# Normalized rows turned by VectorE's 32x32 blocks and a DRAM scratch instead of TensorE's transposes

## The chip, the cores and the metric

The kernel runs on one core of a Trainium2 chip. That core has five engines with instruction queues of their own: TensorE (PE, with its weight loads PEld), VectorE (DVE), ScalarE (ACT), GpSimd (POOL) and SyncE (SP), which here only issues transfers. The transfers run on 16 DMA engines. SBUF is the on-chip memory of 128 partitions, PSUM the accumulator memory of 8 banks into which TensorE writes. The metric is the time of one execution on the device, in microseconds (us).

## What is computed

The reference is one block of a network on x with 2048 rows of 512 values, in f32: softmax attention with 32 heads of 16 values, then a gated MLP that mixes rows.

```python
def _A_ref(x, wqkv, wo):                       # attention, H = 32, Dh = 16
    qkv = (x @ wqkv).reshape(B, S, 3, H, Dh).transpose(2, 0, 3, 1, 4)
    p = softmax(einsum("bhqd,bhkd->bhqk", q, k) * Dh ** -0.5)
    o = einsum("bhqk,bhkd->bhqd", p, v)
    return o.transpose(0, 2, 1, 3).reshape(B, S, D) @ wo

def _B_ref(x, w_in, w_sp, b_sp, w_out):        # F = 1376, Fh = 688
    z = gelu(einsum("bsd,df->bsf", x, w_in))
    z1, z2 = z[..., :Fh], layernorm(z[..., Fh:])
    g = einsum("ts,bsf->btf", w_sp, z2) + b_sp[None, :, None]
    return einsum("bsf,fd->bsd", z1 * g, w_out)

h = x + _A_ref(layernorm(x), wqkv, wo)
out = h + _B_ref(layernorm(h), w_in, w_sp, b_sp, w_out)
```

Each f32 product is made of three products of rounded halves (hi and lo): hi x hi, hi x lo and lo x hi. To *split* a tile below is to make these two halves.

## The kernel before, in words

The 2048 rows are cut into 16 blocks of 128. The kernel has four stages: the projections to q, k and v; the attention; a middle stage, which makes h and z of every block; and the last stage, which mixes the blocks with w_sp and writes the output. The change lies in the end of the attention stage and in the middle stage.

The path of one block (`sb`) through the middle stage is this.

- `load_o` (line 619) asks, on SyncE's queue, for the attention output o of the block, already turned (from the scratch `o_scr`, 256 KB), for the reciprocals of the softmax sums `rc` (four transfers from `r_scr` that repeat each row 16 times), and for the rows of x (`xr`). GpSimd then multiplies o by rc (line 630). The buffers are o and rc two each, xr three.
- `split_o` (line 633) makes the halves of o, one on ScalarE and one on VectorE.
- `make_h` (line 645) is 12 products on TensorE (line 643); `add_h` (line 651) adds x on VectorE, stores h to `h_scr`, and takes statistics; `scale_h` (line 659) makes mean and scale from them.
- `hn`, the normalized row block, is made by ScalarE (line 1097), or by VectorE for the first three blocks (line 883).
- `turn` (line 1010) turns it: four transposes of 128x128 on TensorE (line 1015) into a PSUM tile `tp`, and a split of that tile to `hT`, first half on ScalarE (line 100), second on VectorE (line 105).
- `make_z` (line 1024), three times: 12 products each (lines 108 to 110) into a PSUM tile, and the gelu on ScalarE (line 1034).
- `gate_z` (line 1037) stores both halves of z by ScalarE's queue, normalizes the second (line 1046), calls what it is given as `meanwhile`, and, for blocks 8 to 15, lets GpSimd combine two blocks (lines 1058 to 1066) to the operands of the last stage. The second half of z has five buffers (line 1021).

The blocks are taken in the order 0, 1, 2, 8, 9, 10, 3, 11, 4, 12, 5, 13, 6, 14, 7, 15 (`h_rows`). Below, "row k" is the k-th in this order. Step k of the middle stage makes h of row k + 3, turns row k + 1, makes z of row k, splits o of row k + 4 and asks for o of row k + 5. h and hn of rows 0, 1 and 2 are made earlier, in the last part of the attention stage (`play_final` and `more_h`), where o of rows 3 and 4 is asked for too.

The order is written out by hand: in the last part of the attention stage the queues of TensorE, ScalarE, VectorE and SyncE, and from the middle stage on GpSimd's too, execute in the order of the program text. An instruction that waits holds up all that stands behind it on its engine. In the last part of the attention the order of pieces is the string `FINAL`: G is a score with its exponential, V a product with v, H one of the 12 products of h, T the transfers of the row maxima.

## Time and profile before

| | us |
|---|---|
| median of 3 runs | 1803.15 |
| lowest and highest | 1802.88, 1803.16 |
| the profiled execution | 1802.38 |
| its span | 1800.6 |

| engine | busy us | share of the span | instructions |
|---|---|---|---|
| TensorE (PE) | 1793.1 | 100% | 13371 |
| TensorE weight loads (PEld) | 1050.6 | 58% | 13371 |
| VectorE (DVE) | 1500.0 | 83% | 3034 |
| ScalarE (ACT) | 1378.4 | 77% | 2674 |
| GpSimd (POOL) | 218.4 | 12% | 299 |

The last part of the attention runs from about 1307 to 1351 us of the span, the middle stage from 1351 to 1514 us. The granted clock of TensorE is full throughout.

How to read the rows that follow. A row of the groups names line, engine and operation, then output and inputs with their shapes, the number of instructions, and after the bar the busy us, the mean ns of one, and the idle time of the engine before them with what ended it. A row of the timeline begins with the start and the duration in us; in brackets stands the idle time before it and its releaser. SPq and ACTq rows are transfers being issued on the queues of SyncE and ScalarE; how long the data then takes is not in them. A row of the windows gives for a stretch of time the busy us of PE, PEld, DVE, ACT and POOL with their instructions, the clock, the busy share of the DMA engines and GB/s.

### The profile page before, as it was taken

What the parts mean: (1) busy time and instruction counts of PE and PEld (TensorE: products, weight loads), DVE (VectorE), ACT (ScalarE), POOL (GpSimd) and SP (SyncE); (2) the same over time, 40 slices, a digit from 0 to 9 for tenths busy, and PEclk for the clock granted to TensorE, in tenths of its full rate; (3) what the DMA queues carried; (4) which work ended last, traced back from release to release, by engine and by line L of the source; (5) the groups of instructions that cost most, each with busy time, mean ns of one, the idle gap of its engine ahead of it and who ended that gap; (6) DMA issues with size and microseconds to landing.
All of it is one profiled execution on the core that took longest, in us unless ns stands there. A gap on an engine that the chain in (4) does not pass through costs nothing.

```text
span 1800.6 us, 36057 instructions
## 1 busy us (share of the span) xinstructions
PE 1793.1 (100%) x13371; PEld 1050.6 (58%) x13371; DVE 1500.0 (83%) x3034; ACT 1378.4 (77%) x2674; POOL 218.4 (12%) x299
## 2 busy tenths in 40 slices
PE   9999999999999999999999999999999999999999
PEld 6876444444444444444444444444448889999998
DVE  6487999999999999999999999999936676778664
ACT  3224999999999999999999999999994445334231
POOL 2241000011010100000000000000110754001111
PEclk9999999999999999999999999999999999999999
DMA  6677111221120111021012011100134554668562
GB/s 199 192 194 182 43 26 27 49 56 30 36 59 19 51 39 26 20 50 35 14 36 44 24 30 38 26 15 15 40 74 143 168 176 151 216 208 278 184 197 91
DMA packets 148184, 157.54 MB, mean 87 GB/s; under 512 B 63032, under 2 KB 93256, under 8 KB 146664
## 3 DMA queue, kind: packets, MB, share of 16 engines
q1 hardware_dynamic: 143224, 143.82, 29.6%
q10 hardware_dynamic: 4752, 11.41, 1.6%
q8 instruction: 105, 1.72, 0.4%
q14 instruction: 71, 0.58, 0.1%
q0 software_dynamic: 32, 0.01, 0.0%
HBM read 99.69 MB, written 54.56 MB: 86 GB/s over the span
## 4 chain that ended last, share of the span: by engine, by line
PE 99%; DVE 1%; DMA 0%; issue 0%; ACT 0%; DVEq 0%
PE pv L726 30%; PE s L700 10%; PE s L237 9%; PE m L700 9%; PE m L237 7%; PE acc L108 6%; PE acc L110 6%; PE acc L109 6%; PE g L110 4%; PE g L109 4%; PE g L108 4%; PE acc L643 2%; PE tp L1319 1%; PE h L643 1%; PE acc L1340 0%; PE tp L1015 0%
## 5 line engine op out<-in xcount | busy, mean ns | idle before, releaser
L704 ACT ACTIVATE pt<-s 128x512 f32<-128x512 f32 (+1 forms) x1149 | 668.5, 632 | 3.4 <-PE s L700 3.0
L726 PE MATMUL pv<-pt,vst 128*32 128x256 f32 (+1 forms) x6048 | 595.2, 467 | 0.0
L242 DVE TENSOR_REDUCE mx<-s 128x1 f32<-128x512 f32 x826 | 539.6, 682 | 42.3 <-PE s L237 34.4
L704 ACT ACTIVATE pt<-m 128x512 f32<-128x512 f32 x855 | 500.3, 616 | 0.2 <-PE m L700 0.2
L242 DVE TENSOR_REDUCE mx<-m 128x1 f32<-128x512 f32 x682 | 452.3, 682 | 28.3 <-PE m L237 21.2
L700 PE MATMUL s<-qst,kst 50*128 50x512 f32 x1193 | 418.5, 437 | 0.0
L237 PE MATMUL s<-kst,qst 48*128 48x512 f32 x963 | 343.7, 421 | 0.0
L700 PE MATMUL m<-qst,kst 50*128 50x512 f32 x855 | 340.1, 440 | 0.0
L237 PE MATMUL m<-kst,qst 48*128 48x512 f32 x794 | 290.8, 423 | 0.0
L700 PEld LDWEIGHTS s<-qst,kst 50*128 50x128 f32 x1193 | 187.4, 184 | 145.0 <-DVE mx L242 91.0
L726 PEld LDWEIGHTS pv<-pt,vst 128*32 128x32 f32 x6048 | 120.4, 108 | 217.6 <-issue 208.5
L700 PEld LDWEIGHTS m<-qst,kst 50*128 50x128 f32 x855 | 146.2, 184 | 129.4 <-DVE mx L242 88.9
L237 PEld LDWEIGHTS s<-kst,qst 48*128 48x128 f32 x963 | 166.8, 184 | 40.4 <-issue 12.8
L237 PEld LDWEIGHTS m<-kst,qst 48*128 48x128 f32 x794 | 137.1, 184 | 41.7 <-issue 15.2
L247 ACT ACTIVATE ab<-s 128x512 f32<-128x512 f32 x167 | 100.4, 601 | 14.2
L102 POOL CAST mparts<-nm 128x16 fp32r<-128x16 f32 x32 | 6.3, 196 | 861.3 <-DVE nm L255 861.3
L251 DVE CUSTOM_DVE_ANT_0 ab<-s,ab 128x512 f32<-128x512 f32 x137 | 93.2, 680 | 5.1 <-PE s L237 5.1
L955 ACT ACTIVATE ws<-a 128x512 fp32r<-128x512 f32 x80 | 45.7, 621 | 48.7 <-PE g L110 23.8
L251 DVE CUSTOM_DVE_ANT_0 ab<-m,ab 128x512 f32<-128x512 f32 x112 | 76.2, 680 | 4.9 <-PE m L237 4.9
L237 PE MATMUL s<-dst,qst 48*128 48x512 f32 x167 | 79.6, 477 | 0.0
L1034 ACT ACTIVATE z<-acc 128x464 f32<-128x464 f32 (+2 forms) x64 | 27.5, 456 | 63.5 <-PE acc L110 63.5
L108 PE MATMUL acc<-wi,hT 128*128 128x464 f32 (+2 forms) x196 | 72.8, 371 | 0.0
(219 smaller groups left out, 2586.9 us busy)
## 6 DMA issues: line engine op xcount, KB each, us to landing
a<-in_w_sp SPq DMA_DIRECT2D x80, 256.0 KB
qst<-q_scr SPq DMA_DIRECT2D x192, 64.0 KB
z_scr<-z ACTq DMA_DIRECT2D x32, 344.0 KB
kst<-k_scr SPq DMA_DIRECT2D x42, 256.0 KB
k_scr<-part SPq DMA_DIRECT2D x16, 512.0 KB
q_scr<-part SPq DMA_DIRECT2D x16, 512.0 KB
z<-z_scr SPq DMA_DIRECT2D x14, 344.0 KB
b<-z_scr SPq DMA_DIRECT2D x24, 172.0 KB
```

Source lines behind the costliest of these rows:

```text
L108: nc.tensor.matmul(ps, lh, rh, start=first, stop=False)
L109: nc.tensor.matmul(ps, lh, rl, start=False, stop=False)
L110: nc.tensor.matmul(ps, ll, rh, start=False, stop=last)
L237: nc.tensor.matmul(acc, q[r, p, c], keys[r, p], start=True, stop=True)
L242: nc.vector.reduce_max(at(t, e if t else e - 1), acc, axis=AX.X)
L247: nc.scalar.activation(ab[0], acc, AF.Relu)
L251: nc.vector.tensor_tensor_reduce(ab[0], acc, ab[0], 1.0, LOW, ALU.add, ALU.max, at(0, 0))
L643: yield nc.tensor.matmul(acc, o2[b][:, d, :], wo2[a][:, d, :], start=i == 0, stop=i == 3 * DB - 1)
L700: nc.tensor.matmul(out, kst[hg % 2][r, p, kb * P:(kb + 1) * P], qst[hg * NQ + qb][r, p, :], start=True, stop=True)
L704: nc.scalar.activation(out, scores, AF.Exp, scale=DH ** -0.5)
L726: nc.tensor.matmul(pv[0][32 * j:32 * j + 32, cols], vst[hg % 2][:, c:c + 32], pt[:, places[t, p], cols], start=kb == 0, stop=kb == NB - 1 ...
L955: nc.scalar.activation(hi, src, AF.Copy)
```

## The change

The rows of hn are no longer turned by TensorE. VectorE transposes each 32x32 block of the 128x512 tile in its place (`flip`); four transfers of SyncE write the result to a new DRAM scratch `ht_scr` in pieces of 32 values, so that the blocks come to stand in their turned places; one more transfer reads the turned block back (`fetch_turned`), and it is split from SBUF (`split_turned`).

In step k of the middle stage VectorE transposes row k + 3 behind the statistics of z, `meanwhile` issues the fetch of row k + 2, then the load of o, and last the four writes of row k + 3; row k + 1 is split behind the split of o. o is asked for six rows ahead, row k + 6 instead of k + 5, and o of row 5 at the start of the stage. Rows 0, 1 and 2 are transposed and written in the attention stage, rows 0 and 1 are fetched and row 0 is split there. The two PSUM buffers of `tp` go to the accumulators of `make_z`, which get seven instead of five.

```diff
@@ -90,6 +90,7 @@
     o_scr = dram.tile([D, S], F32, name="o_scr")
     r_scr = dram.tile([H, S], F32, name="r_scr")
     h_scr = dram.tile([S, D], F32, name="h_scr")
+    ht_scr = dram.tile([D, S], F32, name="ht_scr")
     z_scr = [dram.tile([S, FH], F32, name=f"z{i}_scr") for i in range(2)]
     s_scr = dram.tile([HB, P, HB, P], F32, name="s_scr")
     g_scr = [dram.tile([3, P, FC], F32, name=f"g{p}_scr") for p in range(HB)]
@@ -614,7 +615,7 @@
     wi4 = w_in.rearrange("(a p) c -> p a c", p=P)
 
     h_rows = [0, 1, 2, HB, HB + 1, HB + 2] + [sb + HB * i for sb in range(3, HB) for i in range(2)]
-    os_, o2s, xrs, hns, hTs = {}, {}, {}, {}, {}
+    os_, o2s, xrs, hTs = {}, {}, {}, {}
 
     def load_o(sb):
 
@@ -655,6 +656,33 @@
         nc.sync.dma_start(h_scr[sb * P:(sb + 1) * P, :], h)
         hst[sb] = e2.tile([P, 6], F32, name="st")
         nc.vector.bn_stats(hst[sb], h)
+
+    def flip(sb, hn):
+
+        z = e2.tile([P, D], F32, name="hz", tag="hn", bufs=3)
+        nc.vector.transpose(z, hn)
+        q = 32
+
+        def write():
+            for i in range(P // q):
+                c = sb * P + q * i
+                nc.sync.dma_start(ht_scr[:, c:c + q].rearrange("(j r) c -> r j c", r=q),
+                                  z[q * i:q * i + q, :].rearrange("r (j c) -> r j c", c=q))
+
+        return write
+
+    def fetch_turned(sb, pool, **slot):
+
+        raws[sb] = pool.tile([P, DB, P], F32, name="ht", **slot)
+        nc.sync.dma_start(raws[sb], ht_scr[:, sb * P:(sb + 1) * P].rearrange("(a p) s -> p a s", p=P))
+
+    def split_turned(sb, eh=None):
+
+        hTs[sb] = [hT[0][:, i, turns[0] % 2] for i in range(2)]
+        turns[0] += 1
+        split(hTs[sb][0], hTs[sb][1], raws.pop(sb), eh)
+
+    raws, turns, hT = {}, [0], []
 
     def scale_h(sb):
         mv = e2.tile([P, 2], F32, name="mv")
@@ -820,6 +848,8 @@
                             invert()
                         if len(units) in (7, 5):
                             load_o(h_rows[(7, 5).index(len(units)) + 3])
+                        if len(units) in (13, 3):
+                            fetch_turned(h_rows[(13, 3).index(len(units))], e2, tag="rc")
                     unit, pt, p = half
                     for step in score(unit, p, pt):
                         step()
@@ -864,7 +894,7 @@
 
             for _ in range(k):
                 if not pieces:
-                    sb = h_rows[len(hns)]
+                    sb = h_rows[made[0] // (3 * DB)]
                     acc = later[0].tile([P, 512], F32, name="h")
                     pieces.extend([sb, acc, h_products(sb, acc)])
                 sb, acc, products = pieces
@@ -873,15 +903,18 @@
                 if made[0] % (3 * DB):
                     continue
                 pieces.clear()
-                after = h_rows[len(hns) + 1]
+                if made[0] == 6 * DB:
+                    split_turned(h_rows[0])
+                after = h_rows[made[0] // (3 * DB)]
                 o = os_.pop(after)
                 hi, lo = o2s[after] = [e2.tile([P, DB, P], F32R, name=f"o2{i}", bufs=1) for i in range(2)]
                 nc.vector.tensor_copy(hi, o)
                 add_h(sb, acc, lambda: nc.vector.tensor_sub(lo, o, hi.bitcast(F32)))
                 mv, rs = scale_h(sb)
-                hns[sb] = e2.tile([P, D], F32, name="hn", bufs=3)
-                nc.vector.tensor_scalar(hns[sb], xrs.pop(sb), mv[:, 0:1], rs,
+                hn = e2.tile([P, D], F32, name="hn", bufs=3)
+                nc.vector.tensor_scalar(hn, xrs.pop(sb), mv[:, 0:1], rs,
                                         op0=ALU.subtract, op1=ALU.mult)
+                flip(sb, hn)()
 
         made = [0]
         units = [(hg, qb, kb) for hg in range(HG) for qb in range(NQ) for kb in range(NB)]
@@ -919,6 +952,7 @@
                 if n == 482:
                     split_o(h_rows[0], "pool", "pool")
             load_o(h_rows[2])
+            hT.append(wc.tile([P, 2, 2, DB, P], F32R, name="hT", tag="w2"))
             maxima.close()
             for stack in reversed(singles):
                 stack.close()
@@ -1000,22 +1034,8 @@
     with ExitStack() as mid:
         m2 = mid.enter_context(tc.tile_pool(name="mid_2", bufs=2))
         zs, zst = {}, {}
-        hT = wc.tile([P, 2, 2, DB, P], F32R, name="hT", tag="w2")
         ph = mid.enter_context(tc.tile_pool(name="mid_ph", bufs=1, space=PSUM))
-        pt = mid.enter_context(tc.tile_pool(name="mid_pt", bufs=2, space=PSUM))
-        ps = mid.enter_context(tc.tile_pool(name="mid_ps", bufs=5, space=PSUM))
-
-        turned = [0]
-
-        def turn(sb):
-
-            hn = hns.pop(sb)
-            tp = pt.tile([P, DB, P], F32, name="tp")
-            for d in range(DB):
-                nc.tensor.transpose(tp[:, d, :], hn[:, d * P:(d + 1) * P], ident)
-            hTs[sb] = [hT[:, i, turned[0] % 2] for i in range(2)]
-            turned[0] += 1
-            split(hTs[sb][0], hTs[sb][1], tp, "act")
+        ps = mid.enter_context(tc.tile_pool(name="mid_ps", bufs=7, space=PSUM))
 
         def new_z(sb):
             zs[sb] = [m2.tile([P, FH], F32, name=f"z{i}", bufs=1 + 4 * i) for i in range(2)]
@@ -1067,13 +1087,11 @@
 
         w = [Slot(wc, f"w{i}") for i in range(3)]
         row = dict(enumerate(h_rows))
-        turn(row[0])
+        load_o(row[5])
         for k in range(NB):
             sb, new = row[k], row.get(k + 3)
             if new is not None:
                 make_h(new, (ph if k else ps).tile([P, 512], F32, name="acc"))
-            if k + 1 < NB:
-                turn(row[k + 1])
             if new is not None:
                 mv, rs = scale_h(new)
                 nb = minus_mean(e2, mv, rs)
@@ -1089,16 +1107,28 @@
             make_z(sb, *chunks[0])
             if k + 4 < NB:
                 split_o(row[k + 4])
+            if k + 1 < NB:
+                split_turned(row[k + 1], "act")
             make_z(sb, *chunks[1])
             for c in range(2):
                 nc.vector.bn_stats(zst[sb][:, c, :], zs[sb][1][:, c * FC:(c + 1) * FC])
             if new is not None:
-                hns[new] = e2.tile([P, D], F32, name="hn", bufs=3)
-                nc.scalar.activation(hns[new], xrs.pop(new), AF.Identity, bias=nb, scale=rs)
+                hn = e2.tile([P, D], F32, name="hn", bufs=3)
+                nc.scalar.activation(hn, xrs.pop(new), AF.Identity, bias=nb, scale=rs)
+                write = flip(new, hn)
             for c in chunks[2:]:
                 make_z(sb, *c)
             hTs.pop(sb)
-            gate_z(sb, lambda: k + 5 < NB and load_o(row[k + 5]))
+
+            def meanwhile():
+                if k + 2 < NB:
+                    fetch_turned(row[k + 2], m2)
+                if k + 6 < NB:
+                    load_o(row[k + 6])
+                if new is not None:
+                    write()
+
+            gate_z(sb, meanwhile)
             if not k:
                 invert()
             if k == NB - 5:
```

## The prediction

> **What bounds the kernel now.** I read the page first: the busy shares and the chain that ended last.
>
> ```profile
> span 1800.6 us, 36057 instructions
> ...
> PE 1793.1 (100%) x13371; PEld 1050.6 (58%) x13371; DVE 1500.0 (83%) x3034; ACT 1378.4 (77%) x2674; POOL 218.4 (12%) x299
> ...
> PE 99%; DVE 1%; DMA 0%; issue 0%; ACT 0%; DVEq 0%
> ```
>
> TensorE is the chain for 99% of the span. So work taken from TensorE is worth its whole time, as long as everything that feeds TensorE keeps up with the shorter beat. Next the chain in order of time over the stage with the transposes. Its columns are start, us, what.
>
> ```profile
> 1351.36 0.59 PE tp L1015 x4
> ...
> 1383.99 2.76 PE acc L643 x12
> ...
> 1394.66 2.77 PE acc L643 x12
> ...
> 1498.67 0.44 PE tp L1015 x4
> ```
>
> A step with an output-projection row (12 products of L643, four transposes of L1015, 36 products of the gMLP input) lasts 1394.66 - 1383.99 = 10.67 us, with no gap. There are 16 groups of four transposes, the first costing 0.59 us and each later one 0.44 us of the chain. The busy time by step and the groups by line show what the other engines have to spare:
>
> ```profile
> 1383.99:1394.66 10.67, 10.67 (x54) 9.40 (x53) 7.30 (x25) 4.50 (x8) 1.28 (x1) 1.00 0.52 162
> ...
> L1015 PE MATMUL tp<-ident,hn 128*128 128x128 f32 x64 | 9.6, 273 | 0.0
> L135 DVE TENSOR_SCALAR rs_r<-rs_t 128x1 f32<-128x1 f32 x34 | 7.3, 214 | 1.2
> L281 DVE STREAM_TRANSPOSE mturned<-mparts 128x32 f32<-128x32 f32 x32 | 6.5, 204 | 0.6 <-DMA o<-o_scr 0.6
> L105 DVE TENSOR_TENSOR hT<-tp,hT 128x512 fp32r<-128x512 f32 x16 | 10.8, 678 | 5.8 <-ACT hT L100 5.8
> ```
>
> In that step (PE, PEld, DVE, ACT, POOL, clock, DMA share, GB/s) VectorE works 7.30 us, ScalarE 4.50, the DMA engines are 0.52 busy, and the clock is full.
>
> **What the change takes away.** All 64 transposes leave TensorE: 0.59 + 15 x 0.44 = **7.2 us** of the chain. The group's 9.6 us of busy time is an upper bound, because those matmuls overlap their neighbours. The full step becomes 10.67 - 0.44 = 10.23 us. Write S for the start of a step: step 0 still starts at 1351.36, and step k at 1351.36 + 10.23 k while nothing stalls. The splits of hT go on in the same number, and only move behind the split of o. PSUM goes from five and two buffers to seven for the gMLP accumulators, at no price.
>
> **What it adds on VectorE.** One 128x512 block transpose per row, which the trace does not show. It is new work, so no gain is in it: at least the 0.20 us of the 128x32 one, at most 16 times that, 3.26 us. A pass over one element costs 0.214 us (L135), so the 0.204 is nearly all a start that is paid once; I take 0.68 us, the pass over 512 elements. VectorE then has 8.0 of 10.23 us, and at 3.26 it has 10.6, hardly over a step. The place matters more: the transpose stands before the statistics of z, and there VectorE idles before the next add.
>
> ```profile
> 1390.86 0.69 DVE L105 TENSOR_TENSOR o<-o,o 128x512 fp32r<-128x512 f32 x1
> ...
> 1397.47 0.69 DVE L653 TENSOR_TENSOR xr<-acc,xr 128x512 f32<-128x512 f32 x1 [1.72 <-PE acc L643]
> ...
> 1334.27 0.43 DVE L879 CAST o<-o 128x512 fp32r<-128x512 f32 x1 [6.31 <-PE h L643]
> ...
> 1338.49 0.55 DVE L883 TENSOR_SCALAR hn<-xr,mv,rs_r 128x512 f32<-128x512 f32 x1
> ```
>
> The 1.72 us gap covers 0.68; without the cover the add is late by the excess, 1.5 us at 3.26, and what waits for the add is only the next row's statistics. The three transposes and the one split moved into the last attention stage lie in gaps like the 6.31 us before L879; without them ScalarE's exponentials would still not wait, as they read only scores.
>
> **What it adds on the queue of SyncE.** Per step four stores of 64 KB and one fetch of 256 KB. Order in a step: store of h, fetch of a turned row, o, four rc, x, and last the four stores, which wait for the transpose. The rows of before for step 3 on SyncE, and of the slow broadcast reads rc:
>
> ```profile
> 1387.51 0.33 SPq L655 DMA_DIRECT2D h_scr<-xr  x1
> 1387.93 0.39 SPq L623 DMA_DIRECT2D o<-o_scr  x1
> 1388.37 2.47 SPq L626 DMA_DIRECT2D rc<-r_scr  x4
> ...
> 1130.24 1.71 SPq L195 DMA_DIRECT2D raw<-v_scr  x2
> ...
> 1135.64 1.04 POOL L197 COPY vst<-raw 128x1024 f32<-128x1024 f32 x1 [12.22 <-DMA raw<-v_scr]
> ```
>
> At 2.47 / 4 = 0.62 us an issue, five more are 3.1 us beside the present 0.33 + 0.39 + 2.47 and 0.4 for x (as for o), 3.6: 6.7 of 10.23 us, so the queue fits. The stores of 2048 pieces of 128 bytes have no row. The nearest is raw: two loads, 4096 pieces of 128 bytes, and the reader starts 5.4 us after the first issue. I take that as the stores' landing too: issued from about S+9.9 (transpose done), landed by S+15.3, which is 5 us into the next step. The fetch behind them is read a step later, so it has some 8 us to spare.
>
> **Where the moved load bites.** The o of row k+6 goes into the buffer of row k+4, which comes free only when VectorE has made o's low half: 1390.86 + 0.69 is S+7.56, in the new beat S+7.1. Before, the row k+5 was asked for at S+3.9. GpSimd multiplies o by rc, and in its order that stands ahead of the gate work of the same step. So the gate work waits too. These are its rows, with the rows of ScalarE that need the buffers it frees:
>
> ```profile
> 1396.52 1.28 POOL L630 TENSOR_TENSOR o<-o,rc 128x512 f32<-128x512 f32 x1 [9.46 <-DMA rc<-r_scr]
> ...
> 1407.83 1.29 POOL L630 TENSOR_TENSOR o<-o,rc 128x512 f32<-128x512 f32 x1
> ...
> 1430.47 1.30 POOL L630 TENSOR_TENSOR o<-o,rc 128x512 f32<-128x512 f32 x1
> ...
> 1389.75 0.56 ACT L1034 ACTIVATE z<-acc 128x464 f32<-128x464 f32 x1 [1.93 <-PE acc L110]
> ...
> 1432.46 0.56 ACT L1034 ACTIVATE z<-acc 128x464 f32<-128x464 f32 x1 [1.92 <-PE acc L110]
> ...
> 1369.03 2.46 SPq L626 DMA_DIRECT2D rc<-r_scr  x4
> ...
> 1377.81 1.29 POOL L630 TENSOR_TENSOR o<-o,rc 128x512 f32<-128x512 f32 x1 [8.69 <-DMA rc<-r_scr]
> ```
>
> Call L the time from the last rc issue to the multiply: 1396.52 - 1390.84 = 5.7 us in step 3, 1377.81 - 1371.49 = 6.3 in step 1. Three gates in a row (steps 3, 4, 5) keep GpSimd busy from 1396.52 to 1430.47, 33.95 us. The z of step 7 takes the buffer that the third gate frees (five buffers, line 1021), and before it had 1432.46 - 1430.47 = 2.0 us to spare. New: the multiply of step 3 can start at S+7.1 + 2.9 (o and rc issues) + L; the third gate ends at S+43.95 + L; ScalarE wants the buffer at 4 x 10.23 + 5.32 (1389.75 is S+5.76, less 0.44) = S+46.24. So ScalarE waits w = L - 2.3: 3.4 us at L = 5.7. From that activation to o's low half is 1391.55 - 1389.75 = 1.8 us, and the next step's L643 needs it: it tolerates w = 10.23 - 5.32 - 1.8 = 3.1 us. The stall of TensorE is **L - 5.4**, once. Beyond about L = 6.6 the wait in step 5 also delays the o of row 11, and each further microsecond of L counts twice. For L the low end is 5.7 (stall 0.3; none if the reads come faster). The high end: the reads now share the DMA engines with two stores of z, x and the new stores. I take L = 6.5, near the rows, **1.1 us** of stall.
>
> ```profile
> z_scr<-z ACTq DMA_DIRECT2D x32, 344.0 KB
> ```
>
> With x and a turned row, 128x512 f32 each, that is 2 x 344 + 256 + 256 KB = 1.2 MB; at 162 GB/s per 0.52 share, 312 GB/s, all of it ahead of the reads is 4 us: L = 10.3, stall (10.3 - 5.4) + (10.3 - 6.6) = 8.6 us.
>
> **The start of the stage.** Row 5 is now asked for behind the stores of row 2 and the last attention output:
>
> ```profile
> 1350.99 0.55 DVE L883 TENSOR_SCALAR hn<-xr,mv,rs_r 128x512 f32<-128x512 f32 x1
> ...
> 1352.96 0.32 SPq L747 DMA_DIRECT2D o_scr<-o  x1
> ...
> 1357.94 0.51 SPq L748 DMA_DIRECT2D sums<-o  x1
> ...
> 1359.17 0.38 SPq L623 DMA_DIRECT2D o<-o_scr  x1
> ...
> 1370.26 0.68 DVE L105 TENSOR_TENSOR o<-o,o 128x512 fp32r<-128x512 f32 x1
> ```
>
> 1351.54 + 0.7 transpose + 4 x 0.62 issues = 1354.8, the eight transfers 5.5 us, so o at 1360.3, 1.1 us later than 1359.17; o's low half at 1370.94 + 1.1 = 1372.0 at worst, against S of step 2 at 1351.36 + 20.46 = 1371.8. I take **0.4 us**; with a 3.26 us transpose it is up to 2.8, and nothing if VectorE was not waiting for the load there.
>
> **Other loads behind the stores.** Row 4, in the attention stage, now waits for the stores of row 1: 1338.49 + 0.55 + 0.7 + 2.5 = 1342.2, then 2.9 + L + 1.3, ready at 1352.9; its split comes at 1351.36 + 5.9 = 1357.3. Four microseconds cover it. At the end of the stage the third block of spatial weights is issued behind the last stores:
>
> ```profile
> 1483.97 0.93 SPq L961 DMA_DIRECT2D a<-in_w_sp  x2
> ...
> 1490.91 2.54 POOL L975 TENSOR_TENSOR s<-a,a 128x512 f32<-128x512 f32 x2
> ...
> 1509.41 0.93 POOL L956 TENSOR_TENSOR n<-z,n 128x344 fp32r<-128x344 f32 x1
> ...
> 1513.97 0.32 PE L108 MATMUL g<-t,ws 128*128 128x344 f32 x1
> ```
>
> New issue: step 12 at 1474.1 + 12.4 + 1.5 of stalls = 1488, four microseconds later, so GpSimd's differences start about when they did, and its last gate ends near 1510.3 as now. The last stage then begins at 1513.97 - 5.7 = 1508.3, but with the first of that gate's four products; the one that ends at 1510.3 is the last. I put nothing; if TensorE waited for all of it, it is 2 us.
>
> **The sum**: -7.2 + 1.1 + 0.4 = **-5.7 us**. Against the profiled execution, 1802.38 us (1.8 beside its span), that is 1796.7; the median of the runs is 0.8 higher, 1803.15, so 1797.4 us.
>
> **Rival 1: the late multiply eats the gain.** Same mechanism, L of 7.7 to 9.5: stall 3.4 to 7.0 us, gain between 3.4 and -0.2. For it: the reads now run while z is stored. Against it: L was 6.3 at most where stores of z overlapped. Time at L = 8.5: stall 5.0, 1803.15 - 7.2 + 5.0 + 0.4 = 1801.3.
>
> **Rival 2, slower: the 128-byte stores fill the DMA engines.** Place: every step, SyncE waiting for the landing before the fetch, all reads behind. Rows of the DMA queue for 236 to 246 us (the raw loads) and 221 to 228 (r_scr, pieces of 64 bytes written):
>
> ```profile
> q1 hardware_dynamic: 4272, 0.60, 38.8%
> ...
> q1 hardware_dynamic: 192, 0.01, 1.7%
> ```
>
> 0.388 x 160 us / 4272 = 14.5 ns a piece read, 0.017 x 112 / 192 = 10 ns a piece written. At 14.5 the store takes 2048 x 14.5 / 16 = 1.9 us of a step, the fetch 0.8 (256 KB at 312 GB/s), beside the present 0.52 x 10.67 = 5.5: 8.2 of 10.23. It decides from 30 ns a piece, where the sum is the step. At 40 ns the step is 11.5 us: 13 steps x 1.2 = 16 us lost, 1803.15 - 5.7 + 16 = 1813. The rows speak against it, though none writes 128 bytes at an 8 KB pitch. [...]
>
> **Rival 3: it does not do what it says**, because the fetch lands after the split wants it and TensorE waits for hT instead of transposing. From the 8 us to spare, the store and fetch would need more than 13 us together; then each step loses the excess, and 0.5 us a step already returns the 7.2: 1803.
>
> **Chances.** Forecast 0.62 (its own range 1795.4 to 1799.5), rival 1 0.20, rival 2 0.12, rival 3 0.06. A measurement of this kernel tells a change from none at about 0.2%, 3.6 us. Faster needs a gain over 3.6: the forecast and a little of rival 1, 0.64. Same: most of rivals 1 and 3, 0.20. Slower: rival 2 and the tail of rival 1 beyond L = 11, 0.16. The range runs from all hidden with a little more of the 9.6 us, 1795.0, to L = 10.3 with the late row 5: 1803.15 - 7.2 + 8.6 + 0.4 = 1805.0.
>
> **What would show it.** A beat of 10.23 us between the first L643 of two steps, no L1015, GpSimd's first gate about 4 us later in its step than now, ScalarE's L1034 waiting for GpSimd in steps 5 to 7, and a TensorE gap of about a microsecond before step 8: the forecast right. A 128x512 block transpose of 0.6 to 0.8 us; L of 5.7 to 7. Wrong: L643 waiting in every step, DMA share near 1, a gap before L108 that hT's split ends, or new idle of TensorE where the last stage begins.

## The result and the profile after

The change made the kernel slower: 1832.03 us against 1803.16 us, a ratio of 1.0162 (95% interval 1.0150 to 1.0174). The profiled execution took 1832.6 us with a span of 1830.8, 30.2 more than the span before. The forecast of 1797.4 us and its range, 1795 to 1805, are both missed, with the wrong sign.

From the page of the changed kernel, the engines' busy time and the chain that ended last:

```profile
PE 1801.0 (98%) x13307; PEld 1052.0 (57%) x13307; DVE 1512.8 (83%) x3051; ACT 1375.9 (75%) x2673; POOL 220.9 (12%) x299
...
PE 90%; DMA 5%; DVE 2%; SPq 2%; issue 1%; POOL 0%; ACT 0%; ACTq 0%; DVEq 0%; POOLq 0%
```

The 64 transposes are gone (13371 - 13307 = 64 matmuls), but TensorE is no longer the whole chain: transfers and SyncE's queue are in it. In the timeline of TensorE (start, duration, line, in brackets the idle time before and what ended it) the first product of h in each step and the gaps are these; the last row opens the last stage:

```profile
1352.40 3.06 PE L644 MATMUL acc<-wo,o 128*128 128x512 f32 x12
1368.71 5.49 PE L644 MATMUL acc<-wo,o 128*128 128x512 f32 x12 [5.77 <-ACT o L101]
1381.88 2.92 PE L644 MATMUL acc<-wo,o 128*128 128x512 f32 x12
1392.13 2.92 PE L644 MATMUL acc<-wo,o 128*128 128x512 f32 x12
1402.38 2.92 PE L644 MATMUL acc<-wo,o 128*128 128x512 f32 x12
...
1428.04 5.34 PE L644 MATMUL acc<-wo,o 128*128 128x512 f32 x12 [5.01 <-ACT o L101]
...
1486.96 0.48 PE L109 MATMUL acc<-wi,hT 128*128 128x464 f32 x1 [2.00 <-ACT hT L101]
...
1500.44 0.47 PE L111 MATMUL acc<-wi,hT 128*128 128x464 f32 x1 [0.74 <-DVE hT L106]
...
1517.83 0.48 PE L109 MATMUL acc<-wi,hT 128*128 128x464 f32 x1 [2.38 <-ACT hT L101]
...
1533.06 0.65 PE L109 MATMUL acc<-wi,hT 128*128 128x344 f32 x1 [5.78 <-ACT hT L101]
...
1544.11 0.40 PE L109 MATMUL g<-t,ws 128*128 128x344 f32 x1 [0.59 <-issue]
```

Where nothing disturbs it, the step is 1402.38 - 1392.13 = 10.25 us, as forecast. The middle stage lasts 1544.11 - 1352.40 = 191.7 us; before it lasted 1513.97 - 1351.36 = 162.6. The seven gaps are 22.3 us. With the 7.2 us of transposes gone, 162.6 - 7.2 + 22.3 = 177.7; another 14 us are missing. They lie behind the gaps: the 12 products that follow one take 5.49 or 5.34 us where 2.92 is usual. The clock record of the trace has five stretches of that stage at half clock, 27.3 us together, which is a loss of 13.7 us. Stretches of that stage (columns as before: busy time and count of PE, PEld, DVE, ACT, POOL, then the granted clock, the DMA share and GB/s):

```profile
1391.00:1401.00 10.00, 10.00 (x49) 8.79 (x48) 6.75 (x24) 3.50 (x8) 1.29 (x1) 1.00 0.68 195
...
1421.00:1431.00 10.00, 4.99 (x17) 3.60 (x16) 2.91 (x6) 3.24 (x7) 7.21 (x11) 0.76 0.67 130
1431.00:1441.00 10.00, 10.00 (x45) 8.74 (x44) 8.88 (x29) 4.08 (x8) 9.54 (x12) 0.90 0.66 180
...
1531.00:1541.00 10.00, 7.94 (x34) 7.71 (x35) 5.58 (x16) 4.48 (x9) 7.00 (x10) 0.66 0.53 168
```

In these stretches the clock is 1.00 where TensorE had no gap, and 0.66 to 0.90 in the mean of ten microseconds around and after one.

Three different things end the gaps. The queue of SyncE comes first, one round of it:

```profile
1397.14 0.38 SPq L677 DMA_DIRECT2D ht<-ht_scr  x1
1397.57 0.50 SPq L624 DMA_DIRECT2D o<-o_scr  x1
1398.12 2.46 SPq L627 DMA_DIRECT2D rc<-r_scr  x4
1400.67 0.40 SPq L630 DMA_DIRECT2D xr<-in_x  x1
1401.17 4.51 SPq L669 DMA_DIRECT2D ht_scr<-hz  x4
1405.78 0.47 SPq L656 DMA_DIRECT2D h_scr<-xr  x1
1408.78 0.38 SPq L677 DMA_DIRECT2D ht<-ht_scr  x1
1409.22 0.50 SPq L624 DMA_DIRECT2D o<-o_scr  x1
1409.76 2.47 SPq L627 DMA_DIRECT2D rc<-r_scr  x4
```

This round takes 1408.78 - 1397.14 = 11.6 us, more than a step of 10.25. The four stores hold the queue for 4.5 us, and the fetch then waits 2.5 us more. What SyncE waited for between 1372 and 1480 us (total us, times, longest), in the kernel before and in the changed one:

```profile
SPq L655 <- DVE xr L653: 63.4, 10, 6.8
```

```profile
SPq L677 <- DMA ht_scr<-hz: 16.9, 14, 3.0
SPq L669 <- DMA rc<-r_scr: 10.4, 9, 1.8
```

Before, SyncE idled some six us a step, until VectorE had h for it to store. Now it waits for landings: the fetch (L677) for the stores, which it must, and the stores (L669) for rc, which they do not read. The second wait goes with the semaphores that tell of a landing. This kernel's program gives the transfers of SyncE and ScalarE, in one common order, eight semaphores in turn (101, 110, 112 to 116 and 118 in the trace), and a transfer that gets a semaphore may have to wait until the one eight places before it has landed. The semaphore events of the trace show it: each of the 202 transfers that the two queues issued between 1352 and 1544 us went out only after the one before it on its semaphore had landed, and 75 of them name that semaphore as what they wait for. In the round shown, the third read of rc, issued at 1399.38, landed at 1405.36, and the fourth store, which takes over its semaphore, was issued at 1405.38. A piece of that order (place in the program; from the trace, when it was issued, its queue, the transfer, its semaphore, and what it waits for of the same semaphore where it names that one):

```
1099 1392.92 ScalarE  store z, 1st half         112
1100 1393.67 SyncE    store h                   113
1101 1394.98 ScalarE  store z, 2nd half         114
1102 1397.14 SyncE    fetch of a turned row     115  (all stores of that row, the last landed 1397.08)
1103 1397.57 SyncE    o                         116
1104 1398.12 SyncE    rc, the first             118
1105 1398.74 SyncE    rc, the second            101
1106 1399.38 SyncE    rc, the third             110
1107 1400.00 SyncE    rc, the fourth            112  1099, ScalarE's store of z, landed 1396.82
1108 1400.67 SyncE    x                         113
1109 1401.17 SyncE    1st store of a turned row 114
1110 1401.60 SyncE    2nd store                 115  1102, the fetch, landed 1400.20
1111 1403.16 ScalarE  store z, 1st half         116
1112 1403.18 SyncE    3rd store                 118  1104, rc, landed 1402.66
1113 1406.15 ScalarE  store z, 2nd half         101
1114 1405.38 SyncE    4th store                 110  1106, rc, landed 1405.36
```

Before, a step has 9 transfers, so the eighth before is, for all but the last, one of the step before. Now it has 14, and for six of them the eighth before belongs to the same step.

Second, the late o. GpSimd's multiply in step 3, the operation of the gate behind it that frees a buffer of z, and then the gelu on ScalarE that waits for that buffer:

```profile
1417.61 1.29 POOL L631 TENSOR_TENSOR o<-o,rc 128x512 f32<-128x512 f32 x1 [10.29 <-DMA ht_scr<-hz]
...
1425.97 0.91 POOL L1085 TENSOR_TENSOR z<-z,t 128x344 f32<-128x344 f32 x1
```

```profile
1426.91 0.56 ACT L1054 ACTIVATE z<-acc 128x464 f32<-128x464 f32 x1 [9.29 <-POOL z L1085]
```

The split of o, which stands behind that gelu on ScalarE, ends the 5.01 us gap. Third, waits that are neither: at the start of the stage the first gelu, which loads its table, waits for the last transfers of the attention's sums (ScalarE, first row below), and at its end SyncE's stores of the spatial weights' differences, L1031, wait for GpSimd, with the last fetch behind them (SyncE, the other rows).

```profile
1366.29 1.28 ACT L1054 ACT_TABLE_LOAD   x1 [12.16 <-DMA sums<-o]
```

```profile
1527.43 1.55 SPq L1031 DMA_DIRECT2D s_scr<-a  x2
1529.15 0.37 SPq L677 DMA_DIRECT2D ht<-ht_scr  x1
```

### The profile page after: what moved, and what is told of

Read it like the earlier page. It is cut to its first block, busy times and chain, and to the rows that moved or that the text cites. A ratio compares the mean times of both kernels' runs of the same rounds, so it can differ in the third digit from the quotient of the medians.

```text
span 1830.8 us, 36070 instructions
## 1 busy us (share of the span) xinstructions
PE 1801.0 (98%) x13307; PEld 1052.0 (57%) x13307; DVE 1512.8 (83%) x3051; ACT 1375.9 (75%) x2673; POOL 220.9 (12%) x299
## 4 chain that ended last, share of the span: by engine, by line
PE 90%; DMA 5%; DVE 2%; SPq 2%; issue 1%; POOL 0%; ACT 0%; ACTq 0%; DVEq 0%; POOLq 0%
PE pv L754 29%; PE s L728 10%; PE s L238 9%; PE m L728 8%; PE m L238 7%; PE acc L109 4%; PE g L111 4%; PE g L110 4%; PE acc L111 4%; PE g L109 4%; PE acc L110 4%; DMA rc<-r_scr 2%; DMA ht_scr<-hz 1%; PE acc L644 1%; SPq L627 1%
## 5 line engine op out<-in xcount | busy, mean ns | idle before, releaser
L248 ACT ACTIVATE ab<-s 128x512 f32<-128x512 f32 x167 | 100.5, 602 | 14.2
L109 PE MATMUL acc<-wi,hT 128*128 128x464 f32 (+2 forms) x196 | 74.5, 380 | 10.2 <-ACT hT L101 10.2
L111 PE MATMUL acc<-wi,hT 128*128 128x464 f32 (+2 forms) x196 | 75.0, 383 | 0.8 <-DVE hT L106 0.7
```

What stands on the lines that cost most here:

```text
L109: nc.tensor.matmul(ps, lh, rh, start=first, stop=False)
L111: nc.tensor.matmul(ps, ll, rh, start=False, stop=last)
L248: nc.scalar.activation(ab[0], acc, AF.Relu)
```

## The experiments

All times are medians, with the ratio to the kernel before and its 95% interval. Line numbers are those of each run's own text. The theories are: the *queue* (or *series*) theory, that SyncE's round is longer than a step because it waits for landings; the *late-o* theory, the forecast's own mechanism alone; the *small-pieces* theory, that 128-byte pieces fill the DMA engines; and the *room* theory for the first gap. From the fifth run on the queue theory is put sharper, as *eight in turn*. In the last runs this is account (a), and account (b) is that the turned rows cost the time themselves, however many transfers a step has.

### Room for the turned rows

By the built program's addresses, the middle stage's pool of tiles ends at byte 133824 of a partition with the new buffers and at 129728 without; a pool of the attention, which holds the tile that the last transfers read, begins at 131744. The two now overlap, though not in that tile.

```diff
-                    fetch_turned(row[k + 2], m2)
+                    fetch_turned(row[k + 2], ec, bufs=2)
```

> The two 2 KB buffers for turned rows in the middle stage move from that stage's own pool, where they make it reach into memory of the attention stage, to a pool beside the weights. Room theory: the first gelu of the stage (12.16 us idle for the last attention transfers) starts 8 us earlier, the 5.77 us gap of TensorE before step 1 goes, and with it the low clock behind it (step 1 lasts 13.2 us, not 10.25): 1832.0 - 5.8 - 2.9 = 1823. Queue theory: SyncE still needs 12.3 us a step, so a part of that comes back as waits for turned rows, 1823 to 1830. If the gelu waits for these transfers for another reason: 1832.

1830.79 us, 1.0155 (1.0140 to 1.0170). The first gap is gone, so the overlap of the pools caused it:

```profile
1362.68 2.92 PE L644 MATMUL acc<-wo,o 128*128 128x512 f32 x12
...
1426.91 4.91 PE L644 MATMUL acc<-wo,o 128*128 128x512 f32 x12 [8.77 <-ACT o L101]
```

But the time hardly moved: the later gap grew from 5.01 to 8.77 us. That is just above the queue theory's range: what TensorE is given early, SyncE's round takes back.

### The fetch behind the loads, and o five rows ahead

```diff
+                if k + 6 < NB:
+                    load_o(row[k + 6])
                 if k + 2 < NB:
                     fetch_turned(row[k + 2], m2)
-                if k + 6 < NB:
-                    load_o(row[k + 6])
```

> In each step the fetch of a turned row is issued behind the loads of o, rc and x instead of ahead of them; all else as in the changed kernel. Queue theory (SyncE works through fetch, loads, stores and two waits for landings in series, 12.3 us): the wait for the stores' landing, 3.0 to 3.9 us, now passes while the loads are issued, a round takes about 9 us and TensorE sets the beat of 10.25 us again; the waits of the hT split go (9 of them, 34.6 us). What stays is the first gap: 1803.2 - 7.2 + 5.8 + 2.9 + 1.5 = 1806. Late-o theory (the forecast's mechanism alone): o comes 3 to 4 us earlier, the 5.0 us gap before step 6 shrinks to 1 to 2 us, the others stay: 1825. Small-pieces theory (the DMA engines are short of time): no byte is saved, 1830 or more.

1848.56 us, 1.0255 (1.0240 to 1.0270): slower still, which none of my theories said. Its rounds on SyncE,

```profile
1409.48 0.38 SPq L624 DMA_DIRECT2D o<-o_scr  x1
1409.96 8.71 SPq L627 DMA_DIRECT2D rc<-r_scr  x4
...
1423.99 0.38 SPq L624 DMA_DIRECT2D o<-o_scr  x1
```

and its longest waits between 1340 and 1600 us:

```profile
SPq L627 <- DMA z_scr<-z: 43.2, 9, 6.3
```

A round is now 1423.99 - 1409.48 = 14.5 us, and 8.7 of them pass in issuing four reads of rc. They wait for ScalarE's store of z, which rc has nothing to do with; in that program's order the fourth rc now has the semaphore of z's store of the same step. The series is not the one that I had drawn, and moving one transfer changes who waits for whom.

```diff
-        load_o(row[5])
...
-                if k + 6 < NB:
-                    load_o(row[k + 6])
+                if k + 5 < NB:
+                    load_o(row[k + 5])
```

> o is loaded five rows ahead as before the change, row 5 in step 0 again; the rest as in the changed kernel. Late-o theory: GpSimd's multiply is early, the gates are early, the gap of 5.0 us before step 6 goes, and the time falls to about 1810 (the first gap alone stays). Queue theory: SyncE's series per step is as long as it was, 12.3 us; the gap before step 6 may go, but the hT split waits for the fetch in more steps instead: 1822 to 1832. Small-pieces theory: about 1827.

1846.20 us, 1.0239 (1.0224 to 1.0254), also above all ranges. Asking for o a row earlier does not make it early: now the stores wait for z (SyncE's L669 for z_scr, 31.6 us in eight waits), o and rc come late by the queue, and TensorE waits for o's split in 11 steps, 22.2 us.

### Large pieces instead of small ones

```diff
-                nc.sync.dma_start(ht_scr[:, c:c + q].rearrange("(j r) c -> r j c", r=q), ...)
+                nc.sync.dma_start(ht_scr[c:c + q, :], z[q * i:q * i + q, :])
```

> The four stores and the fetch move the same bytes through a scratch laid out so that the stores write pieces of 2 KB instead of 128 bytes; the fetch still reads pieces of 512 bytes. The turned order of the elements is left out, so the gMLP works on wrongly ordered rows; every instruction stays. Small-pieces theory: the stores are issued in 2.5 us instead of 4.4 to 5.8 and land in under 2 us, SyncE's round falls under 10.25 us and the time to about 1806. Queue theory: the stores still wait for the rc landing (5.7 us after its issue) and the fetch for the stores; the round falls by 1 us at most: 1824 to 1832.

1826.54 us, 1.0134 (1.0117 to 1.0151). Small pieces cost 5.5 us of the 29; not the cause, but more than nothing. The fetch's waits for the stores sum to 17.5 us over the stage, where the changed kernel has 23.6.

### Transfers alone, on the kernel before

```diff
+                    for i in range(5 * k, 5 * k + 5):
+                        nc.sync.dma_start(tiny[i:i + 1, :], ident[0:1, 0:32])
```

> The kernel before, and in each of the 13 steps that make a row of h, five stores of 128 bytes each (one row of the identity to a scratch that nobody reads), last on SyncE: 14 transfers a step on the queues of SyncE and ScalarE as in the changed kernel, not 9, but no bytes and nothing that depends on them. Eight-in-turn theory (the built program lets a transfer start only when the one eight places before it, on either queue, has landed): SyncE, which in before waits only for VectorE's sum (63.4 us in ten steps), waits for landings of z, rc and o instead; o and rc come later; 1803 to 1812. Small-pieces theory and late-o theory: 1803 and no such waits.

1803.06 us, 0.9999 (0.9989 to 1.0008). SyncE does wait for landings now (L656, the store of h, 15.4 us for x in ten steps), and TensorE doesn't notice. So 14 transfers a step are harmless by their number alone, when the five added ones are tiny and nothing needs them.

```diff
+                write = flip(new, hns[new])     # transpose and four stores, nobody reads them
```

> The kernel before, and in each of the 13 steps also VectorE's block transpose and the four stores of 64 KB in pieces of 128 bytes, last on SyncE; nobody reads them, TensorE keeps its transposes and o comes five rows ahead: 13 transfers a step. Eight-in-turn theory: much as with five tiny stores, or a little later because these land later: 1803 to 1815, SyncE waiting for landings. Small-pieces theory: the DMA engines pay for 2048 pieces a step, clearly more than with the tiny stores, 1815 or more. If the waits of the reading side alone were to blame: 1803 and SyncE still idle for several us a step.

1805.74 us, 1.0014 (1.0005 to 1.0024): 2.5 us for 13 rows. All packets and those of SyncE's queue (packets, MB, share of the 16 DMA engines) between 1380 and 1480 us, first in the kernel before and then in this run, give the price of a piece:

```profile
DMA packets 14999, 16.74 MB, mean 167 GB/s; under 512 B 1063, under 2 KB 9861, under 8 KB 14991
...
q1 hardware_dynamic: 12399, 10.30, 38.2%
```

```profile
DMA packets 33314, 18.26 MB, mean 183 GB/s; under 512 B 19454, under 2 KB 28670, under 8 KB 33305
...
q1 hardware_dynamic: 30674, 11.72, 54.3%
```

16.1% of 16 engines for 100 us is 258 us, for 18391 pieces more of under 512 bytes: 14.0 ns each (the records of the 128-byte packets themselves have 13.0 in the median in the changed kernel's trace, same stretch). The prediction took 14.5 from another row. The stores in themselves, then, cost little. That the fetch, which must follow them, and what stands behind it make the rest is argued: no run adds the fetch alone.

### The stores on other queues

GpSimd issues them, ahead of its multiply, with the room, the fetch behind and o five ahead:

```diff
-                nc.sync.dma_start(ht_scr[:, c:c + q] ...
+                nc.gpsimd.dma_start(ht_scr[:, c:c + q] ...
```

> The changed kernel with its four stores issued by GpSimd, ahead of its multiply, on its own queue with its own semaphores; o five rows ahead, the fetch behind the loads, and the buffers of turned rows beside the weights. The pieces stay 128 bytes. 10 transfers a step are left on the two shared queues. Eight-in-turn theory: SyncE's round falls to 6 or 7 us, its waits for landings go, and the waits of the hT split with them; GpSimd, busy for 33.95 us with three gates in a row, gets four issues of about 0.7 us more a step, so its gates come late and cost a gap or two: 1803.2 - 7.2 + 4 to 8 = 1800 to 1806. Small-pieces theory: 1825 or more.

1822.43 us, 1.0107 (1.0092 to 1.0122), between the two theories. GpSimd's queue, to which that run's program gives semaphores of its own, issues the four in 2.6 us without a wait, but GpSimd was full:

```profile
1414.87 2.61 POOL L669 DMA_DIRECT2D ht_scr<-hz  x4
1417.49 1.28 POOL L631 TENSOR_TENSOR o<-o,rc 128x512 f32<-128x512 f32 x1
...
1429.06 2.60 POOL L669 DMA_DIRECT2D ht_scr<-hz  x4
```

In the steps with gates its round is 1429.06 - 1414.87 = 14.2 us. I had counted the 2.6 us a step, but put a gap or two on it; it sets the beat of those steps.

ScalarE issues them behind its second store of z, first with nothing else altered, then with all orders mended (the buffers of the turned rows beside the weights, o five rows ahead, the fetch behind the loads; the same with the stores on SyncE is the run of the next section, which the second expectation calls the last one):

```diff
-                write = flip(new, hn)
+                write = flip(new, hn, nc.scalar)
```

> The changed kernel with one thing altered: in the middle stage ScalarE issues the four stores, behind its second store of z at the end of the step, where it idles until the next gelu; fetch first, o six rows ahead, small pieces and 14 transfers a step stay. Series theory (SyncE's round is long because stores, which wait for rc to land, and the fetch, which waits for the stores to land, stand in one queue): the round falls below 10.25 us, the late waits of the hT split go; the first gap (room), its low clock and one stall for the late o stay: 1803.2 - 7.2 + 5.8 + 2.9 + 1 to 3 = 1806 to 1808. Theory that the stores or the count of transfers cost the time on whatever queue: 1825 or more.

1840.55 us, 1.0209 (1.0194 to 1.0224), as the second theory has it: ScalarE's gelu waits for the stores (L1054, 63.7 us in 12 waits between 1340 and 1560 us).

> As the last one, but ScalarE issues the four stores at the end of the step. Series theory: no queue has a series longer than a step; beat 10.25 us, no gap of TensorE: 1803.2 - 7.2 = 1796, up to 1799 where a wait stays. Theory that the stores cost the time on whatever queue: 1825 or more.

1851.55 us, 1.0275 (1.0260 to 1.0291). Here ScalarE does the waiting:

```profile
1411.11 7.72 ACTq L669 DMA_DIRECT2D ht_scr<-hz  x4
1418.88 0.56 ACT L1054 ACTIVATE z<-acc 128x464 f32<-128x464 f32 x1 [8.24 <-DMA ht_scr<-hz]
```

Four issues take 7.7 us and the gelu behind them is late. The theory that one long series on one queue is to blame falls: the semaphores are common to both queues, so the wait goes with the transfers.

### All orders mended, stores on SyncE

> The changed kernel with all three orders mended and the stores left on SyncE: buffers of turned rows beside the weights, o five rows ahead, fetch behind the loads. Series theory: rc still waits for the stores and for ScalarE's stores of z, the stores for rc; as with the fetch alone moved, the round is longer than 10.25 us, 1830 to 1845. If the order of loads, fetch and room were all there is to it: 1797.

1852.24 us, 1.0274 (1.0259 to 1.0289), above its range. Room, order and distance of o are not enough; rc waits for z as in the run with the fetch behind the loads (39.8 us in seven waits between 1372 and 1480 us).

### Fewer transfers

The changed kernel with rc in one transfer of plain rows:

```diff
-            nc.sync.dma_start(rc[:, d, :], r_scr[8 * d:8 * d + 8, c] ... .to_broadcast([8, DH, P]))
+        nc.sync.dma_start(rc, o_scr[:, c].rearrange("(d p) s -> p d s", p=P))
```

> The changed kernel with the four broadcast reads of the reciprocals rc replaced by one read of 256 KB (a second copy of the o block, so the division by the softmax sums is left out and h is wrong): the same bytes into the buffer, 11 transfers a step, not 14. Eight-in-turn theory: the stores no longer wait for the landing of rc (10.4 us in ten steps), 1.9 us of issues go, SyncE's round falls from 12.3 to 8.6 us, TensorE sets the beat of 10.25 us; the first gap and one stall of about a microsecond stay: 1806. Small-pieces theory: 1828. Late-o theory: o and rc land 2 us earlier, 1826.

1811.20 us, 1.0045 (1.0030 to 1.0060): 20.8 of 29 us returned. What is left is a first gap of 2.51 us, one of 7.36 at the end of the stage, and the low clock behind them.

The end of the stage, in the changed kernel, with rows 14 and 15 turned by TensorE as before:

> The changed kernel with the last two rows turned by TensorE as before (their stores and fetches go); PSUM is five and two buffers again. The last two gaps of the stage (2.37 and 5.77 us, hT behind a fetch that stands on SyncE behind the stores of the spatial weights' differences) go, and the low clock behind them, about 2 us each; 0.9 us of transposes come back: 1832 - 8.1 - 4 + 0.9 = 1821. If the wait for those stores is hidden behind the same loop anyway: 1828 to 1832.

1817.32 us, 1.0080 (1.0065 to 1.0095): 14.7 us less, more than expected; the last two gaps go with their clock, and the stage runs into the next without one. The ten transfers of these two rows go from the queue too, so not all of it need be the wait for the differences.

Both together, and all orders mended:

> The kernel with all orders mended and the stores on SyncE (1852 us), but rc read in one transfer as in the run with one rc (the division by the softmax sums is left out), and the last two rows turned by TensorE: 11 transfers a step, the same pieces, stores and fetch. Account (a): the round of SyncE is shorter than a step, no gaps: 1802.8 - 7.2 + 0.9 = 1796.5, up to 1800. Account (b): 1840 or more.

1796.63 us, 0.9967 (0.9955 to 0.9980). With the division restored, by storing each reciprocal sixteen times so that rc is read like o:

```diff
-            nc.sync.dma_start(r_scr[head(hg, j % 2, j // 2), cols] ...
+            h = head(hg, j % 2, j // 2)
+            nc.sync.dma_start(r_scr[h * DH:(h + 1) * DH, cols].rearrange("o (p c) -> p o c", c=16),
+                              rc[32 * j:32 * j + 32, :] ... .to_broadcast([32, DH, 16]))
```

> As the run with one rc and all orders mended, but with the division: when the softmax sums are inverted, each reciprocal is stored sixteen times, so that a block of reciprocals lies in the scratch like a block of o and is read in one transfer of 512-byte pieces. 11 transfers a step, 14 rows turned by VectorE and the scratch, two by TensorE. Account (a): 1802.6 - 7.2 + 0.9 = 1796.3, up to 1799 if the larger stores in the attention stage cost something. Account (b): 1840 or more.

1797.24 us, 0.9970 (0.9958 to 0.9982): the version that beats both, by 0.3%. TensorE has no gap in the stage, and the beat is 10.25 us, 0.02 over the forecast:

```profile
1392.61 2.92 PE L643 MATMUL acc<-wo,o 128*128 128x512 f32 x12
1402.86 2.92 PE L643 MATMUL acc<-wo,o 128*128 128x512 f32 x12
```

SyncE waits for ScalarE's stores of z here too (L668, 53.4 us in 12 waits between 1340 and 1560 us). But it is the stores of the turned row that wait, and o, rc, x and the fetch of that step are issued before them: a long wait costs nothing where nothing urgent stands behind it.

> The control: the kernel before with the reciprocals stored sixteen times and read in one transfer, 6 transfers a step and not 9; TensorE turns all rows. TensorE has no gap in before, so fewer transfers can give it nothing: 1802.6, within 1 us on both accounts. If it were much faster, the gain of e16 would not be that of the turned rows.

1803.07 us, 1.0001 (0.9992 to 1.0010): the other read of rc gives the kernel before nothing, so the gain is that of the turned rows.

Half of the rows, with stores by GpSimd only where it has no gate:

> Eight of the 16 rows (places 0, 1, 3, 4, 5, 9, 11, 13 in the order of the rows) are turned the new way, the others by TensorE as before. In the middle stage GpSimd issues the stores, only in steps in which it has no gate; fetch behind the loads, o five rows ahead, buffers beside the weights: 9 or 10 transfers a step on the shared queues. Eight-in-turn account (a): no gap; 0.59 + 7 x 0.44 = 3.7 us saved, 1802.8 - 3.7 = 1799, up to 1801. Account (b): each turned row costs what it cost in the changed kernel, about half of the 29 us: 1815.

1804.48 us, 1.0012 (1.0003 to 1.0021): nearer to account (a). The largest gap is 2.51 us, where o's split waits for a multiply that stands behind three gates and GpSimd's four stores; with the clock behind it and smaller gaps it took more than the 3.7 us.

```profile
1434.59 2.60 POOL L670 DMA_DIRECT2D ht_scr<-hz  x4
1437.19 1.27 POOL L632 TENSOR_TENSOR o<-o,rc 128x512 f32<-128x512 f32 x1
```

The last run separates number from kind. It is the version above, with rc read in four plain transfers:

```diff
-        nc.sync.dma_start(rc, r_scr[:, c].rearrange("(d p) s -> p d s", p=P))
+        for d in range(DB):
+            nc.sync.dma_start(rc[:, d, :], r_scr[d * P:(d + 1) * P, c])
```

> The kernel of the last-but-one run (reciprocals stored sixteen times, all orders mended, last two rows by TensorE), but with the block of reciprocals read in four transfers of 64 KB and not one of 256 KB: the same bytes from the same places in the same 512-byte pieces, 14 transfers a step and not 11. Account (a), eight in turn: the fourth read of rc waits again for ScalarE's store of z of the same step, SyncE's round is about 14 us, and the time is back near the 1852 us that four broadcast reads gave, less what the last two rows cost there: 1830 to 1845. If it was the broadcast reads themselves that were slow (their landing, 5.7 us, or their pieces), and not their number: 1797 to 1800.

1805.06 us, 1.0013 (1.0003 to 1.0022). Neither the number of reads nor their kind is enough alone. The number of transfers costs 7.8 us: the fourth read of rc waits for z again (24.7 us in ten waits between 1372 and 1480 us), and TensorE in half of the steps for o. Most of the rest is the kind of read. Against the run with all orders mended, four plain reads save 1852.2 - 1805.1 = 47 us; the last two rows, which TensorE turns here, are an estimated 15 of them (the 14.7 of their own run), which leaves some 32. How the landing shows: on the kernel before, the multiply starts 8.2 us after the first broadcast read is issued (1396.52 - 1388.37), and with one plain read 1392.06 - 1388.37 = 3.7, in the timeline of the control (SyncE and GpSimd):

```profile
1388.37 0.51 SPq L625 DMA_DIRECT2D rc<-r_scr  x1
...
1392.06 1.30 POOL L628 TENSOR_TENSOR o<-o,rc 128x512 f32<-128x512 f32 x1 [9.52 <-DMA rc<-r_scr]
```

With four reads in both runs, one broadcast read takes 4.7 us in the median from its issue to its landing with all orders mended (31 reads between 1372 and 1482 us, by the semaphore events of the trace), and one plain read in the last run 3.0 (40 reads). In the kernel before, between the same times, a broadcast read of 64 KB takes 5.5 (36 reads) and the plain read of o, with 256 KB, 2.8 (nine reads). All 36 broadcast reads make nine such events each, the reads of o sixteen; no run shows why.

This fits an account in which the eight in turn and the slow landing multiply each other: each late landing holds a semaphore that an unrelated transfer needs. How the 29 us of the changed kernel divide exactly stays open, since the shares overlap: 14.7 us come back with the two last rows, 20.8 with one plain rc, 5.5 with large pieces, about one with the room, and these add up to more than 29.

### A gap by itself

Twelve copies on ScalarE in one step of the kernel before:

```diff
+            if k == 6:
+                for _ in range(12):
+                    nc.scalar.activation(pad, wo2[0][:, 0, :].bitcast(F32), AF.Copy)
```

> The kernel before with twelve copies of 128x512 on ScalarE ahead of the split of o in step 6, about 7 us, that nobody reads: TensorE gets one gap before step 7, of 7 us less the 3.1 us that it can wait, about 4 us, and nothing else is altered. If the low granted clock behind the gaps of the changed kernel comes of the gaps themselves, it is seen here too (about 0.8 to 0.9 for some 20 us) and the time is 2 to 4 us more than the gap: 1803.2 + 4 + 3 = 1810. If not, the clock stays full behind it: 1807.

1809.35 us, 1.0036 (1.0024 to 1.0049), as expected. TensorE's timeline and one stretch of that stage:

```profile
1431.32 4.69 PE L643 MATMUL acc<-wo,o 128*128 128x512 f32 x12 [4.04 <-ACT o L100]
1443.77 2.93 PE L643 MATMUL acc<-wo,o 128*128 128x512 f32 x12
```

```profile
1430.00:1440.00 10.00, 8.69 (x34) 6.96 (x35) 7.49 (x23) 5.41 (x11) 1.89 (x2) 0.83 0.35 118
```

The gap is 4.0 us, and the step behind it 12.45 us instead of 10.68: a gap of 4.0 costs 5.8.

## Why the prediction was wrong, point by point

**What is taken away**: right. The beat is 10.25 us (10.23 forecast), and without gaps the kernel takes 1797.2 us with 14 rows turned the new way.

**VectorE's transpose**: right. The 16 take 0.69 us in the median (0.68 forecast), and in the middle stage nothing waits for one.

**The queue of SyncE**: the step that failed. "6.7 of 10.23 us, so the queue fits" added up how long issues take and treated the queue as if it waited for nothing. The issues of fetch, o, rc and x came out at or under the forecast in sum (0.38 + 0.50 + 2.46 + 0.40, for which 0.62 + 0.39 + 2.47 + 0.4 were taken), but the stores took 4.5 us, not 2.5. In the round shown, 1.7 us of this is the fourth store's wait for rc; the second store's issue alone took 1.54 us, where the other three took 0.30 to 0.54, and no run shows why. The fetch then waited 1.8 to 3.3 us for the stores, with o and rc queued behind it. "The fetch behind them is read a step later, so it has some 8 us to spare" is true of the reader, not of the queue in which the fetch stands. The rounds average 12.3 us, and the loop through rc, stores and fetch has no slack in it. That a transfer of this kernel can wait for the eighth before it could be read from its program before the change; the profile before gives little sign of it (SyncE's 63.4 us of waiting there are for VectorE), as with 9 a step the eighth has landed.

**The late o**: the mechanism was right and shows (gelu waits for GpSimd, 9.29 us). L was 1417.61 - (1409.76 + 2.47) = 5.4 us, against 6.5 taken. What failed is the start: the o of step 3 was expected at S + 7.1; it was issued at 1409.22, and S, the start of step 3, was 1392.13, so S + 17.1. The first gate is late, not the third, and the gap is 5.01 us, not 1.1. This error is the queue's.

**Row 5 and the start of the stage**: 0.4 us forecast (its rows, 1372.0 against 1371.8, give 0.2), a 5.77 us gap found, for a reason that the prediction had not looked at: with the new buffers the stage's pool reaches into one of the attention's, and its first gelu waits 12.16 us for the last transfers that read the older pool. With room made, the first steps keep their beat, so row 5 itself costs nothing.

**Other loads, end of the stage**: "I put nothing", 2 us at worst. The prediction looked at the weights behind the stores and not at the fetch behind SyncE's wait for GpSimd's differences, a wait that stood in before and had nothing urgent behind it. Without the transfers of the last two rows the kernel takes 14.7 us less, the clock included.

**Missing from the sum**: the clock. Every stall was priced at its own length. Against 1803.2 - 7.2 = 1796.0 the changed kernel lost 36 us, and 14 of them are low clock.

**The rivals.** Rival 1 did not come: it took L as 7.7 to 9.5, and L was 5.4 in step 3; o was late because it was asked for late. Rival 2 is refuted: pieces cost 14.0 ns, far from the 30 at which it decides, and the version without gaps has DMA engines 0.80 busy (0.72 in the changed kernel). Rival 3 came nearest, TensorE waiting for hT, but by queueing, not because store and fetch took 13 us: from issue to landing a store took 5.6 us and a fetch 3.0 in the median. Of the signs named as wrong, two came: a gap that hT's split ends, and idle time at the end of the stage.

## What to carry to other kernels

A queue's load is its issues and its waits: before a transfer is added to a step, list for it and for all behind it what must have landed first, and count how many transfers lie between two uses of the same semaphore (eight places here, with 14 transfers a step). A wait that is harmless in before, with nothing urgent behind it, is a trap for whatever is queued there later (14.7 us here, with the transfers of the last two rows); so is a new buffer with which a pool reaches into one that an earlier stage still reads (here the first gap, 5.77 us). Where added transfers hurt, shorten the slowest landing in the loop and merge transfers before moving any (here one read of rc instead of four gave back 20.8 us).

## What the runs showed of the hardware

In these runs TensorE's granted clock fell behind some short gaps, and not behind others as long. Behind 4.04 us the next 12 products took 4.69 us instead of 2.93, behind 5.01 and 5.77 us 5.34 and 5.49, and in the run with o five ahead 4.60 behind a gap of 2.03 but 3.29 behind one of 2.22. No run shows why the last two differ.

In the clock record of the changed kernel's trace the middle stage has five stretches at 0.50, and 1.00 between them:

| gap of TensorE, us | its length | clock 0.50 from | for |
|---|---|---|---|
| 1362.94 to 1368.71 | 5.77 | 1368.08 | 6.83 |
| 1423.03 to 1428.04 | 5.01 | 1426.10 | 6.83 |
| 1484.96 to 1486.96 | 2.00 | 1487.54 | 3.41 |
| 1499.70 to 1500.44 | 0.74 | none | |
| 1515.45 to 1517.83 | 2.38 | 1518.26 | 3.41 |
| 1527.28 to 1533.06 | 5.78 | 1531.92 | 6.83 |
| 1543.52 to 1544.11 | 0.59 | none | |

In the 3.41 us ahead of each of these five starts TensorE idled 3.41, 3.07, 2.00, 2.38 and 3.41 us; between 1361.25 and 1364.66, with 1.73 us of idle time, the clock stayed at 1.00 behind it, to 1368.08.
